# The opening of an attention + SwiGLU + max-out kernel: its stages in one written order

## The chip, the cores and the metric

One NeuronCore of a Trainium2 chip. The metric is the device time of the kernel on that core, in microseconds (us): the median over runs. Engines: PE (TensorE: matmuls, transposes), DVE (VectorE), ACT (ScalarE), POOL (GpSimd), SP (SyncE, which here only issues DMA transfers).

## The reference

```python
def _attn_ref(q, k, v):            # 4 batches, 8 heads, 576 positions, head size 64
    scores = (1 / sqrt(D)) * q @ k.T
    rel = pos[:, None] - pos[None, :]
    mask_local = (rel >= 0) & (rel < 32)                       # heads 0 to 3
    mask_strided = (rel >= 0) & (pos[None, :] % 32 == pos[:, None] % 32)   # heads 4 to 7
    attn = softmax(where(mask, scores, -1e9))
    return attn @ v
x = attn_out.transpose(0, 2, 1, 3).reshape(2304, 512)
x = (silu(x @ w_gate) * (x @ w_val)) @ w_out                   # 512 -> 1536 -> 512
return max(x @ w1, x @ w2, x @ w3) @ w_out2                    # 512 -> 768 -> 512
```

The inputs and weights are 32-bit floats; the weights arrive as 64-bit words, of which the kernel makes 32-bit floats itself.

## The kernel before, in words

**The whole.** The 2304 tokens are 72 rows of 32. A first stage works on five chunks of rows (`ROWS`: 16, 14, 14, 14, 14 rows, chunk c = 0 to 4): attention writes a chunk of x, then for each of `NF` = 12 slices f of the hidden width come a gate product (`emit_gate`), a value product (`emit_val`) and an output product (`emit_out`, one slice behind). A second stage does the max-out products from memory. To keep precision, PE works on pairs: a number is split into a high part (rounded, fp32r) and a low part (the rest), and `product` (lines 522 to 527) makes three matmuls of two pairs: high x high (line 525), high x low (526), low x high (527). A gate or value product of chunk 0 is 4 contraction slices (`k`; 0 and 1 hold the local heads, 2 and 3 the strided ones) x 3 = 12 matmuls of 128x512. For chunk 0 the gate uses tanh (line 548) and the output product plain fp32 (line 575); later chunks use Silu.

**Weights.** `order` lists 36 tiles g0, v0, g1, v1, o0, g2, v2, o1, ... (gate, value, output of slice f). A tile is loaded as raw 64-bit words (`load`, line 159, 512 KB, four buffers `raw_p`), converted (`convert`: two passes on ACT, lines 170 and 171; two on POOL, 172 and 173; two on DVE, 174 and 175) and split (`split_w`: high part on ACT, line 147, low part on DVE, line 150; v and o tiles are also written to memory for the later chunks). `weight_step` does one load, one conversion and one split; it is called `LEADW` times before chunk 0's products and three times in each of chunk 0's slices.

**The opening.** Chunk 0's attention is eight blocks (line 780 on): four of strided heads (blocks 0 to 3, 384 KB of loads each), four of local heads (blocks 4 to 7, 512 KB each). A block goes through `scores` (PE, line 311), `softmax` (on DVE masked reductions, line 323; on ACT four exponentials, line 327; on DVE the inverse of the sums, 330 and 331; on POOL the scaling, 332), `transpose` (PE, line 337; the eviction on ACT, 340, or DVE, 342) and `pv` (PE, line 351; then the high part of x on ACT, 357, and its low part on DVE, 359). A strided block has two units, and each is written into x by an operation of its own. After the eight blocks come the first weight steps, and already the first two blocks of chunk 1 (`loct` tiles, scores in line 315). Chunk 1's and 2's attention is spread over the slices of chunk 0 (`fill`); chunk 2's strided rows are done on DVE (`Unit.qk`, lines 437 and 440).

**What sets the order.** The kernel is written as a program, and a scheduler that models the engines' times chooses each engine's order from it when the kernel is built; `tc.issue_after` ties an instruction behind another. Before, one such tie keeps the reductions of the early blocks in the order of the blocks. The PSUM bank pool `gv` has two buffers for gate and value products: a gate product of f + 1 needs the bank that DVE's gate operation of f (line 549) has read last.

## Time and profile before

| | |
|---|---|
| median of 3 runs | 835.55 us (834.53 to 835.9) |
| the profiled execution | 833.92 us, of which its span is 832.1 |
| PE busy | 801.3 us, 96% of the span |
| DVE, ACT, POOL busy | 537.1, 368.0, 249.7 us |
| DMA moved | 202.84 MB, mean 244 GB/s |
| chain of work that ended last | PE 67%, DVE 10%, DMA 4%, ACT 4% |

The profile is one execution; its times are from the start of its span. "Busy" is time in which an engine had an instruction; instructions overlap a little, so the distance between two starts is often shorter than one duration. "Idle before <- X" says what ended the idle time in front of an instruction.

### The profile page before, as it was taken

What the parts mean: (1) busy time and instruction counts of PE and PEld (TensorE: products, weight loads), DVE (VectorE), ACT (ScalarE), POOL (GpSimd) and SP (SyncE); (2) the same over time, 40 slices, a digit from 0 to 9 for tenths busy, and PEclk for the clock granted to TensorE, in tenths of its full rate; (3) what the DMA queues carried; (4) which work ended last, traced back from release to release, by engine and by line L of the source; (5) the groups of instructions that cost most, each with busy time, mean ns of one, the idle gap of its engine ahead of it and who ended that gap; (6) DMA issues with size and microseconds to landing.
All of it is one profiled execution on the core that took longest, in us unless ns stands there. A gap on an engine that the chain in (4) does not pass through costs nothing.

```text
span 832.1 us, 12634 instructions
## 1 busy us (share of the span) xinstructions
PE 801.3 (96%) x4404; PEld 708.2 (85%) x4404; DVE 537.1 (65%) x1094; ACT 368.0 (44%) x834; POOL 249.7 (30%) x252
## 2 busy tenths in 40 slices
PE   4799999999999999899999999999999999999997
PEld 3666666688998889898899999999999989989986
DVE  2888889985956799979996573714644344614440
ACT  4967676334453744726542443523244122512321
POOL 1546655011231233412332465511222031402110
PEclk9999999999999999999999999999999999999999
DMA  8779989976574898577769899798666374744502
GB/s 224 230 229 337 308 270 322 386 235 205 174 239 169 248 297 298 175 262 237 260 217 353 270 374 365 230 386 339 229 246 220 137 242 177 263 155 173 194 0 76
DMA packets 73895, 202.84 MB, mean 244 GB/s; under 512 B 8584, under 2 KB 37896, under 8 KB 70248
## 3 DMA queue, kind: packets, MB, share of 16 engines
q1 hardware_dynamic: 73688, 201.91, 70.9%
q8 instruction: 35, 0.57, 0.3%
q14 instruction: 28, 0.23, 0.1%
q10 hardware_dynamic: 144, 0.13, 0.0%
HBM read 160.33 MB, written 41.68 MB: 243 GB/s over the span
## 4 chain that ended last, share of the span: by engine, by line
PE 67%; DVE 10%; DMA 4%; ACT 4%; issue 3%; SPq 1%; POOL 0%; DVEq 0%; ACTq 0%
PE ps_a L634 13%; PE ps_z L708 8%; PE ps_c L634 7%; PE ps_v L525 4%; PE ps_v L527 4%; PE ps_v L526 4%; PE ps_y L525 4%; PE ps_y L526 4%; PE ps_y L527 4%; PE ps_g L525 3%; PE ps_g L526 3%; PE ps_g L527 3%; PE ps_b L634 3%; DVE pr L437 1%; DVE pr L459 1%
## 5 line engine op out<-in xcount | busy, mean ns | idle before, releaser
L150 POOL TENSOR_TENSOR hl<-ht,hh 128x448 fp32r<-128x448 f32 x48 | 59.8, 1247 | 202.4 <-ACT hh L147 183.5
L150 POOL TENSOR_TENSOR hl<-t,hh 128x384 fp32r<-128x384 f32 x36 | 37.5, 1045 | 207.0 <-ACT hh L147 166.9
L634 PE MATMUL ps_a<-yhT,wr 128*128 128x384 f32 x324 | 94.5, 338 | 2.5 <-ACT s L648 2.5
L525 PE MATMUL ps_g<-xh,wh_g 128*128 128x448 f32 (+1 forms) x240 | 91.9, 383 | 4.0 <-DVE ht L549 2.7
L525 PE MATMUL ps_v<-xh,w_v 128*128 128x448 f32 (+1 forms) x240 | 90.9, 379 | 2.3 <-DVE ht L556 2.3
L526 PE MATMUL ps_g<-xl,wh_g 128*128 128x448 f32 (+1 forms) x240 | 89.5, 373 | 1.5 <-DVE xl L359 1.5
L527 PE MATMUL ps_v<-xh,w_v 128*128 128x448 f32 (+1 forms) x240 | 89.2, 372 | 0.0
L526 PE MATMUL ps_v<-xl,w_v 128*128 128x448 f32 (+1 forms) x240 | 89.1, 371 | 0.0
L527 PE MATMUL ps_g<-xh,wl_g 128*128 128x448 f32 (+1 forms) x240 | 89.0, 371 | 0.0
L648 ACT ACTIVATE s<-ps_a 128x384 f32<-128x384 f32 x81 | 39.3, 490 | 98.2 <-PE ps_a L634 98.0
L526 PE MATMUL ps_y<-hl,w_o 128*128 128x448 f32 x192 | 70.6, 368 | 0.0
L172 POOL TENSOR_SCALAR raw<-raw 128x512 f32<-128x512 f32 x60 | 55.7, 930 | 49.3 <-ACT w L170 26.6
L527 PE MATMUL ps_y<-hh,w_o 128*128 128x448 f32 x192 | 70.4, 366 | 0.0
L147 ACT ACTIVATE hh<-ht 128x448 fp32r<-128x448 f32 x48 | 27.7, 578 | 90.1 <-DVE ht L556 84.9
L708 PE MATMUL ps_z<-wo2t,hh 128*128 128x512 f32 x216 | 64.8, 392 | 0.9 <-ACT osb L726 0.7
L525 PE MATMUL ps_y<-hh,w_o 128*128 128x448 f32 x192 | 65.5, 370 | 0.1
L556 DVE SCALAR_TENSOR_TENSOR ht<-ht,ps_v 128x448 f32<-128x448 f32 (+1 forms) x60 | 37.6, 626 | 40.6 <-PE ps_v L527 25.4
L634 PEld LDWEIGHTS ps_a<-yhT,wr 128*128 128x128 f32 x324 | 59.7, 188 | 3.8 <-ACT s L648 3.2
L174 DVE SCALAR_TENSOR_TENSOR w<-w,raw 128x512 int32<-128x512 int32 x60 | 44.1, 738 | 17.1 <-POOL raw L172 9.2
L525 PEld LDWEIGHTS ps_g<-xh,wh_g 128*128 128x128 f32 x240 | 45.1, 188 | 11.5 <-DVE ht L549 4.4
L634 PE MATMUL ps_a<-ylT,wr 128*128 128x384 f32 x162 | 54.8, 338 | 0.0
L525 PEld LDWEIGHTS ps_v<-xh,w_v 128*128 128x128 f32 x240 | 45.1, 188 | 7.8 <-DVE ht L556 3.2
(134 smaller groups left out, 1880.6 us busy)
## 6 DMA issues: line engine op xcount, KB each, us to landing
wr<-wsdr SPq DMA_DIRECT2D x27, 1792.0 KB, 7.5
raw<-in_w_dram SPq DMA_DIRECT2D x60, 512.0 KB, 5.2
w_v<-wvdr SPq DMA_DIRECT2D x48, 512.0 KB, 4.5
w_o<-wodr SPq DMA_DIRECT2D x48, 512.0 KB, 4.7
wsdr<-whi SPq DMA_DIRECT2D x27, 256.0 KB, 3.6
wvdr<-w_v SPq DMA_DIRECT2D x12, 512.0 KB, 4.4
wodr<-w_o SPq DMA_DIRECT2D x12, 512.0 KB, 6.1
wsdr<-w SPq DMA_DIRECT2D x18, 256.0 KB, 3.5
```

The costliest lines, as they stand in the source:

```text
L147: a = nc.scalar.activation(hi, src, AF.Copy)
L150: return a.ins, lo_eng.tensor_tensor(lo, src, f32(hi), ALU.subtract).ins
L172: nc.gpsimd.tensor_scalar(f32(hi), f32(hi), -0.0, 1.0, ALU.mult, ALU.mult)
L174: nc.vector.scalar_tensor_tensor(w, w, 3, hi, ALU.logical_shift_left, ALU.bitwise_xor)
L437: eng.tensor_tensor(pv, self.k[:, 0:i + 1, :], self.q[:, r:r + 1, :].to_broadcast([128, i + 1, D]), ALU.mult)
L525: nc.tensor.matmul(ps, wh, xh, start=first, stop=False)
L526: nc.tensor.matmul(ps, wh, xl, start=False, stop=False)
L527: nc.tensor.matmul(ps, wl, xh, start=False, stop=last)
L556: m = nc.vector.scalar_tensor_tensor(t, t, 1.0 if c > 0 else 0.5, ps[:, :n], ALU.mult, ALU.mult).ins
L634: nc.tensor.matmul(ps, wts[:, c, a, ks], y[k][b], start=first and k == q == 0, stop=k == 1 and q == 2, skip_group_check=True,)
L648: nc.scalar.activation(s, self.a, AF.Copy)
L708: nc.tensor.matmul(z[j], a[:, ts], w[:, f, b], start=f == q == 0, stop=f == NF2 - 1 and q == 2)
```

## The change

The stages of a block and of a weight tile become steps of their own (`least`, `exps`, `inverse`, `normalise`, `turn`, `evict`, `outputs`, `high`, `low`; `size`, `rounding`, `sign`, `clamp`, `shift`, `rounded`, `high_w`, `low_w`). A string `OPENING` lists the steps of the eight blocks, of the loads, of the first five weight tiles (indices 0 to 4: g0, v0, g1, v1, o0) and of the first gate product, one letter a step, and within `tc.manual_schedule()` they are issued in that order. The first gate product is made in two halves: contraction slices 2 and 3 (`g0`), then 0 and 1 (`g1`). `LEADW` falls from 8 to 5: with the five tiles of the string, as many tiles are converted (11) and split (10) ahead of chunk 0's slices in the program as before. The two units of a strided block are written into x by one operation each for the high and the low part, in chunk 0 and chunk 1 (chunk 1's products are then 56 columns wide and not 64). The tie between the early reductions goes; a new one puts the first `qk` of chunk 2 behind the last low part issued before it.

```diff
-LEADW = 8
+LEADW = 5
...
+OPENING = """
+l0 k0 l1 l2 l3 l4 r0 l5 l6 l7 r1 r2 r3 S0 M0 E0 S1 R0 M1 N0 S2 E1 T0 M2 V0 R1 S3 E2 N1 P0 M3 T1 H0
+R2 E3 L0 S4 N2 T2 M4 V1 a0 R3 P1 V2 N3 E4 c0 T3 P2 s0 V3 R4 S5 H1 t0 r4 q0 P3 L1 N4 H2 M5 H3 T4 L2
+E5 S6 L3 d0 M6 h0 R5 V4 S7 o0 E6 P4 N5 M7 g0 E7 R6 N6 T5 q2 T6 R7 V5 a1 N7 H4 P5 s1 V6 L4 q1 T7 c1
+P6 H5 t1 V7 L5 a2 P7 d1 H6 c2 a3 L6 H7 s2 h1 L7 s3 q3 g1 t2 a4 o1 q4 d2 c3 h2 s4 t3 o2 d3 c4 h3 t4
+o3 d4 h4 o4
+"""
+FIRST = 5
...
-    def convert(key):
-
-        raw = raws.pop(key)
-        hi, lo = raw[:, :, 1], raw[:, :, 0]
+    def size(key):
+        nc.scalar.activation(f32(words(key)[1]), f32(raws[key][:, :, 1]), AF.Abs, scale=2.0 ** -80)
+
+    def rounding(key):
+        nc.scalar.activation(words(key)[0], raws[key][:, :, 0].bitcast(U32), AF.Copy, scale=2.0 ** -29)
+
+    def sign(key):
+        hi = f32(raws[key][:, :, 1])
+        nc.gpsimd.tensor_scalar(hi, hi, -0.0, 1.0, ALU.mult, ALU.mult)
+        eng.tensor_scalar(w, w, W_MAX, W_MIN, ALU.min, ALU.max)
+
+    def shift(key):
         nc.vector.scalar_tensor_tensor(w, w, 3, hi, ALU.logical_shift_left, ALU.bitwise_xor)
+
+    def rounded(key):
+        q, w = made.pop(key)
         nc.vector.tensor_tensor(w, w, q, ALU.add)
         cvt[key] = f32(w)
+    def convert(key):
+        for step in (size, rounding, sign, clamp, shift, rounded):
+            step(key)
+
+    def high_w(key):
...
+        nc.scalar.activation(wt[key][0], cvt[key], AF.Copy)
+
+    def low_w(key, lo_eng):
         w32 = cvt.pop(key)
-        split(*wt[key], w32, nc.scalar, lo_eng)
+        hi, lo = wt[key]
+        lo_eng.tensor_tensor(lo, w32, f32(hi), ALU.subtract)
...
         def softmax(self, norm_eng):
-            sm, mx, sums, ng = self.sm, self.mx, self.sums, 2 * self.nu
-            with ExitStack() as tied:
-                if early_order[0] is not None and self.early:
-                    tied.enter_context(tc.issue_after(early_order[0]))
-                for g in range(ng):
-                    early_order[0] = nc.vector.tensor_tensor_reduce(
-                        sm[:, g], self.s[:, g], self.masks[g // 2], -SCALE, 3.0e38, ALU.add, ALU.min, mx[:, g:g + 1]
-                    ).ins
-            for g in range(ng):
+            self.least()
+            self.exps()
+            self.inverse()
+            self.normalise(norm_eng)
+
...
-            parts = list(self.dst(ps[:, :2 * nu * QB].rearrange("p (a m) -> p a m", a=2)))
-            for hi, lo, src in parts:
+            self.parts = list(self.dst(ps[:, :2 * nu * nq].rearrange("p (a m) -> p a m", a=2)))
+
+        def high(self):
+            for hi, lo, src in self.parts:
                 nc.scalar.activation(hi, src, AF.Copy)
-            for hi, lo, src in parts:
-                nc.vector.tensor_tensor(lo, src, f32(hi), ALU.subtract)
+
+        def low(self):
+            for hi, lo, src in self.parts:
+                last_low[0] = nc.vector.tensor_tensor(lo, src, f32(hi), ALU.subtract).ins
...
-            for u, n in enumerate(g):
-                r0 = min(n * nr, STRIDE - nr)
-                su = src[:, :, u * QB:u * QB + nr * rows].rearrange("p a (r i) -> p a r i", i=rows)
-                for c, i0, i1, o in pieces(b * NI, b * NI + rows):
-                    def part(t):
-                        t = t[:, 2:4, :width(c)].rearrange("p a (i r) -> p a r i", r=STRIDE)
-                        return t[:, :, r0:r0 + nr, i0:i1]
-
-                    xh, xl = x_tile(c)
-                    yield part(xh), part(xl), su[:, :, :, o:o + i1 - i0]
-
-        return Block(srcs, (g[0], g[0]), rows * nr, [smask[b]] * len(g), dst, early)
+            su = src.rearrange("p a (r i) -> p a r i", i=rows)
+            for c, i0, i1, o in pieces(b * NI, b * NI + rows):
+                def part(t):
+                    t = t[:, 2:4, :width(c)].rearrange("p a (i r) -> p a r i", r=STRIDE)
+                    return t[:, :, g[0] * nr:(g[-1] + 1) * nr, i0:i1]
+
+                xh, xl = x_tile(c)
+                yield part(xh), part(xl), su[:, :, :, o:o + i1 - i0]
+
+        return Block(srcs, (g[0], g[0]), rows * nr, [smask[b]] * len(g), dst, early, rows * nr)
...
             steps[s0].append(lambda blk=blk: (blk.scores(), blk.softmax(eng)))
             steps[s0 + 1].append(lambda blk=blk: blk.transpose(nc.scalar))
             steps[s0 + 2].append(blk.pv)
+        def queued(step, n, r, eng):
+            if not (c == 2 and n == 0 and r == 0):
+                return step(r, eng)
+            with tc.issue_after(last_low[0]):
+                step(r, eng)
...
-                steps[s0 + (2 * r // u.n)].append(lambda u=u, r=r: u.qk(r, eng))
+                steps[s0 + (2 * r // u.n)].append(lambda n=n, u=u, r=r: queued(u.qk, n, r, eng))
...
+        return silu(c, f, ps)
+
+    def silu(c, f, ps):
+        n = width(c)
...
-        nc.sync.dma_start(cst, shape_consts)
-        for i, blk in enumerate(blocks):
-            blk.load()
-            if i in RAW_AT:
-                step_load(n_load[0] + 1)
-        lag = 4
-        for i in range(len(blocks) + lag):
-            if i < len(blocks):
-                blocks[i].scores()
-                blocks[i].softmax(nc.gpsimd)
-            if len(blocks) - 2 <= i < len(blocks):
-                step_cvt()
-            if i >= lag:
-                blocks[i - lag].transpose(nc.vector if i % 3 == 2 else nc.scalar)
-                blocks[i - lag].pv()
-        step_split(nc.gpsimd)
-        step_split(nc.gpsimd)
+        gate = []
+
+        def gate_part(ks):
+            if not gate:
+                gate.append(gv.tile([128, 512], F32, name="ps_g", tag="gv"))
+            (xh, xl), (wh, wl), ps = xt[0], wt["g", 0], gate[0][:, :width(0)]
+            for k in ks:
+                c = slice(k * 128, (k + 1) * 128)
+                product(ps, wh[:, c], wl[:, c], xh[:, k, :width(0)], xl[:, k, :width(0)], k == NK // 2, k == NK // 2 - 1)
+
+        def evictor(i):
+            return nc.vector if i % 3 == 2 else nc.scalar
+
...
+            "g": lambda i: gate_part(range(NK // 2, NK) if i == 0 else range(NK // 2)),
+        }
+        with tc.manual_schedule():
+            for step in OPENING.split():
+                steps[step[0]](int(step[1:]))
+        n_cvt[0] = n_split[0] = FIRST
...
-            t = emit_gate(c, f)
+            t = emit_gate(c, f) if s else silu(c, f, gate[0])
```

In the order that the scheduler makes of it, ACT has 36 loads of its function table where there were 30; the six more lie behind chunk 0. Three places of the opening, in the orders of the instructions before and now (line numbers are each kernel's own):

SP, the loads of blocks 2 to 4 (`qe`, `ke`, `ve`) and of the first raw weight tile (`raw`). Before:

```order
L299 DMA qe_162<-in_st0q_dram 128x256
L300 DMA ke_164<-in_st0k_dram 128x256
L301 DMA ve_163<-in_st0v_dram 64x512
L159 DMA raw_170<-in_w1_dram 128x1024
L299 DMA qe_172<-in_st0q_dram 128x256
L300 DMA ke_174<-in_st0k_dram 128x256
```

Now:

```order
L335 DMA ve_165<-in_st0v_dram 64x512
L333 DMA qe_172<-in_st0q_dram 128x256
L334 DMA ke_174<-in_st0k_dram 128x256
L335 DMA ve_173<-in_st0v_dram 64x512
L333 DMA qe_180<-in_earq_dram 128x256
L334 DMA ke_182<-in_lock_dram 128x384
L335 DMA ve_181<-in_locv_dram 96x512
L168 DMA raw_188<-in_w1_dram 128x1024
```

The raw tile has moved behind blocks 3 and 4.

PE, from the last blocks to the first value product (lines 345/311 scores, 388/337 transposes, 409/351 outputs, 349/315 scores of chunk 1, 592 to 594/525 to 527 products). Before:

```order
L351 MATMUL ps_a_491<-qe_188,ve_189 64x64 x8
L337 MATMUL ps_a_519<-cst_105,sme_208 96x128 x4
L315 MATMUL ps_a_820<-loct_814 128x96 x4
L351 MATMUL ps_a_508<-qe_196,ve_197 64x64 x8
L351 MATMUL ps_a_525<-qe_204,ve_205 64x64 x8
L315 MATMUL ps_a_842<-loct_836 128x96 x4
L525 MATMUL ps_g_684<-xh_329,wh_g0_536 128x512
L525 MATMUL ps_v_714<-xh_329,w_v0_540 128x512
L526 MATMUL ps_g_684<-xl_330,wh_g0_536 128x512
```

Now:

```order
L409 MATMUL ps_a_455<-qe_180,ve_181 64x64 x8
L592 MATMUL ps_g_469<-xh_301,wh_g0_435 128x512
...
L594 MATMUL ps_g_469<-xh_301,wl_g0_436 128x512
L388 MATMUL ps_a_483<-cst_105,sme_194 96x128 x4
...
L349 MATMUL ps_a_815<-loct_809 128x96 x4
L409 MATMUL ps_a_537<-qe_206,ve_207 64x64 x8
L349 MATMUL ps_a_837<-loct_831 128x96 x4
L592 MATMUL ps_g_469<-xh_301,wh_g0_435 128x512
```

Six matmuls of the first gate product now stand ahead of block 5's transposes, six behind chunk 1's scores.

ACT, from the last high part of x on (lines 417/357), with the passes over raw tiles (179 and 182/170 and 171), weight high parts (215/147), exponentials of chunk 1's blocks (367/327) and the tanh (619/548). Before:

```order
L357 ACTIVATE xh_329<-ps_a_525 128x2x128
L327 ACTIVATE sm_838,stat_837<-sm_838,stat_837 128x96 x4
L147 ACTIVATE wh_g1_568<-w32_549 128x512
L170 ACTIVATE w32_575<-raw_556 128x512
...
L171 ACTIVATE q_602<-raw_572 128x512
L147 ACTIVATE w_v1_582<-w32_561 128x512
L548 ACTIVATE ht_697<-ps_g_684 128x512
```

Now:

```order
L417 ACTIVATE xh_301<-ps_a_537 128x2x128
L215 ACTIVATE w_v0_555<-w32_500 128x512
L182 ACTIVATE q_549<-raw_218 128x512
L179 ACTIVATE w32_568<-raw_390 128x512
L182 ACTIVATE q_567<-raw_390 128x512
L367 ACTIVATE sm_811,stat_810<-sm_811,stat_810 128x96 x3
L367 ACTIVATE sm_833,stat_832<-sm_833,stat_832 128x96 x3
L619 ACTIVATE ht_692<-ps_g_469 128x512
```

The tanh had all of chunk 1's early exponentials and three raw tiles ahead of it; now the fifth raw tile (`raw_390`) and six exponentials stand ahead of it. On DVE, in the same stretch, chunk 0's last low part now stands ahead of the reductions of the second chunk-1 block, and the shift and the low half of w_v0 (`w_v0_555`) behind them.

## Rows read from the trace of the kernel before

**Rows 1.** Busy time by stage: length, then PE, PEld, DVE, ACT, POOL, clock, DMA.

```profile
0.00:37.45 37.45, 22.15 (x305) 18.59 (x305) 19.21 (x108) 25.55 (x100) 12.28 (x21) 0.95 0.81 224
37.45:47.59 10.14, 6.88 (x32) 5.25 (x32) 10.11 (x26) 7.06 (x19) 5.42 (x6) 1.00 0.64 194
47.59:160.00 112.41, 110.39 (x543) 76.44 (x544) 98.97 (x197) 70.87 (x165) 53.47 (x58) 1.00 0.91 312
160.00:460.00 300.00, 296.88 (x1630) 265.84 (x1629) 243.12 (x498) 143.44 (x308) 80.23 (x77) 1.00 0.74 244
```

**Rows 2.** Waits of PE up to 47.6 us: in total, times, longest.

```profile
PE ps_a L311 <- DMA ke<-in_st0k_dram: 10.5, 4, 6.0
```

**Rows 3.** PE in order of time: start, duration, line, [idle before <- releaser].

```profile
39.70 0.50 PE L526 MATMUL ps_g<-xl,wh_g 128*128 128x512 f32 x1 [1.52 <-DVE xl L359]
...
42.33 0.39 PE L526 MATMUL ps_v<-xl,w_v 128*128 128x512 f32 x1
...
44.59 0.39 PE L527 MATMUL ps_v<-xh,w_v 128*128 128x512 f32 x1
...
47.59 0.50 PE L525 MATMUL ps_g<-xh,wh_g 128*128 128x512 f32 x1 [1.74 <-DVE ht L549]
...
58.25 0.50 PE L525 MATMUL ps_g<-xh,wh_g 128*128 128x512 f32 x1
```

**Rows 4.** The same: the scores of blocks 2 and 3.

```profile
9.17 1.12 PE L311 MATMUL ps_a<-ke,qe 64*64 64x64 f32 x16 [0.55 <-DMA ke<-in_st0k_dram]
13.82 1.12 PE L311 MATMUL ps_a<-ke,qe 64*64 64x64 f32 x16 [3.53 <-DMA ke<-in_st0k_dram]
```

**Rows 5.** ACT in order of time, opening.

```profile
7.38 0.35 ACT L327 ACTIVATE sme<-sme,state 128x64 f32<-128x64 f32 x1 [5.37 <-DVE state L323]
...
23.28 0.61 ACT L357 ACTIVATE xh<-ps_a 128x128 fp32r<-128x128 f32 x2
23.69 0.66 ACT L170 ACTIVATE w<-raw 128x512 f32<-128x512 f32 x1
24.26 0.67 ACT L171 ACTIVATE q<-raw 128x512 int32<-128x512 uint32 x1
...
28.19 0.36 ACT L327 ACTIVATE sme<-sme,state 128x96 f32<-128x96 f32 x1
...
28.55 0.57 ACT L340 ACTIVATE qe<-ps_a 64x512 f32<-64x512 f32 x1
...
37.00 0.39 ACT L357 ACTIVATE xh<-ps_a 128x256 fp32r<-128x256 f32 x1
```

**Rows 6.** DVE in order of time: low parts, a reduction, the shift of a weight.

```profile
22.76 0.71 DVE L359 TENSOR_TENSOR xl<-ps_a,xh 128x128 fp32r<-128x128 f32 x2 [0.73 <-ACT xh L357]
...
36.31 0.68 DVE L174 SCALAR_TENSOR_TENSOR w<-w,raw 128x512 int32<-128x512 int32 x1
...
37.69 0.25 DVE L323 CUSTOM_DVE_ANT_0 sm<-ps_a,cst 128x96 f32<-128x96 f32 x1
...
39.23 0.42 DVE L359 TENSOR_TENSOR xl<-ps_a,xh 128x256 fp32r<-128x256 f32 x1
...
43.77 1.09 DVE L174 SCALAR_TENSOR_TENSOR w<-w,raw 128x512 int32<-128x512 int32 x1
```

**Rows 7.** The last load of chunk 1's two early blocks; landing times of their six loads.

```profile
23.45 0.49 SPq L301 DMA_DIRECT2D loct<-in_locv_dram  x1
...
DMA to landing us min/median/max: 8.4/9.0/9.1
```

**Rows 8.** Busy time and clock around 31 us, columns as in rows 1.

```profile
26.00:31.00 5.00, 2.03 (x33) 1.39 (x32) 4.40 (x18) 4.71 (x18) 2.44 (x3) 1.00 0.78 196
31.00:34.50 3.50, 3.50 (x43) 3.35 (x37) 3.50 (x6) 3.50 (x9) 2.80 (x3) 0.52 0.73 248
```

**Rows 9.** Table loads in front of Silu (busy, mean ns); longest PE wait in 160 to 400.

```profile
L546 ACT ACT_TABLE_LOAD x15 | 19.2, 1283 | 4.2 <-PE ps_g L527 4.0
...
PE ps_v L525 <- DVE ht L556: 2.1, 1, 2.1
```

More of the change, by code (lines that the diff above doesn't have):

```diff
@@ L254, in tile_attention_swiglu_maxout, with __init__ @@
     early_banks = [0]
-    early_order = [None]
+    last_low = [None]
     class Block:
-        def __init__(self, src, at, nk, masks, dst, early=False):
+        def __init__(self, src, at, nk, masks, dst, early=False, nq=QB):
             self.src, self.at, self.nk, self.masks, self.dst = src, at, nk, masks, dst
-            self.nu = len(masks)
+            self.nu, self.nq = len(masks), nq
             self.early = early
@@ L508, in attention_steps @@
         s0 = 0
-        for u in units:
+        for n, u in enumerate(units):
             steps[s0].append(u.load)
@@ L527, in product, with linear @@
         nc.tensor.matmul(ps, wl, xh, start=False, stop=last)
-    def linear(ps, w, x, n):
+    def linear(ps, w, x, n, ks=range(NK)):
         xh, xl = x
-        for k in range(NK):
-            ks = slice(k * 128, (k + 1) * 128)
-            product(ps, w[0][:, ks], w[1][:, ks], xh[:, k, :n], xl[:, k, :n], k == 0, k == NK - 1)
+        for k in ks:
+            c = slice(k * 128, (k + 1) * 128)
+            product(ps, w[0][:, c], w[1][:, c], xh[:, k, :n], xl[:, k, :n], k == ks[0], k == ks[-1])
     hs = {}
@@ new lines, in tile_attention_swiglu_maxout @@
+        steps = {
+            "l": lambda i: blocks[i].load(),
+            "S": lambda i: blocks[i].scores(),
+            "M": lambda i: blocks[i].least(),
+            "E": lambda i: blocks[i].exps(),
+            "R": lambda i: blocks[i].inverse(),
+            "N": lambda i: blocks[i].normalise(nc.gpsimd),
+            "T": lambda i: blocks[i].turn(),
+            "V": lambda i: blocks[i].evict(evictor(i)),
+            "P": lambda i: blocks[i].outputs(),
+            "H": lambda i: blocks[i].high(),
+            "L": lambda i: blocks[i].low(),
+            "r": lambda i: step_load(i + 1),
+            "a": lambda i: size(order[i]),
+            "q": lambda i: rounding(order[i]),
+            "s": lambda i: sign(order[i]),
+            "c": lambda i: clamp(order[i]),
+            "t": lambda i: shift(order[i]),
+            "d": lambda i: rounded(order[i]),
+            "h": lambda i: high_w(order[i]),
+            "o": lambda i: low_w(order[i], nc.vector),
+            "k": lambda i: nc.sync.dma_start(cst, shape_consts),
+            "g": lambda i: gate_part(range(NK // 2, NK) if i == 0 else range(NK // 2)),
+        }
```

65 lines of the change are left out of this document (48 added, 17 removed).

## Prediction

> **What bounds the kernel now.** I read the stages first [rows 1]: from 47.59 us on PE is busy 110.39 of 112.41 us, and then 296.88 of 300; in the 37.45 us before, it is busy 22.15, and between 37.45 and 47.59 it is busy 6.88 of 10.14. So time can be gained in the opening, where PE waits, and after it a microsecond comes only from doing less on PE. The waits of PE up to there [rows 2] name the loads of the strided blocks first, 10.5 us. The order of time on PE [rows 3] gives marks, and shows DVE as what ended the last two waits: the first gate product (f = 0, 12 matmuls) runs without a break from 39.70, the value product's last matmul starts at 44.59, the gate product of f = 1 starts at 47.59 and that of f = 2 at 58.25. From 42.33 to 44.59 there are ten spacings: 0.226 us a matmul. The sum is the shift of these marks.
>
> **The change, part by part.**
>
> *Loads.* The first raw weight tile (512 KB, 524 kB in bytes) moves from behind block 2 to behind block 4. Block 2's scores start at 9.17 and block 3's at 13.82 after a wait of 3.53 [rows 4]. At the opening's 224 GB/s [rows 1] the tile is 2.3 us, so blocks 3 and 4 come 2.3 earlier; everything behind block 4 has the same bytes ahead of it and lands when it did. The constants' 220 KB pass behind block 0's loads: DVE's masks need both, so the first reduction starts as before.
>
> *ACT up to the last early high part.* ACT carries most in the opening: 25.55 us busy in the first 37.45 [rows 1], 24.3 of them after its table load (1.28, as in [rows 9]), between the first exponential at 7.38 and the end of the last high part at 37.39 [rows 5]; it idled 5.7. In the written order it has, before the last high part (H7): 3 exponentials less (0.36 each), one conversion pass less (0.57, from 23.69 to 24.26), one weight high part less (the same size, 0.57), one eviction more (0.57, some 0.5 from start to start), and four strided pairs of high parts as single operations (0.61 becomes the 0.39 of a 128x256 one, 0.22 less each) [rows 5]. That is 2.6 less: 21.7 us. Never idle, ACT would end H7 at 7.4 + 21.7 = 29.1; with the old idle time of 5.7, at 34.8. I take 2.5 of idle time, nearer the lower end, because 2.3 of the old idle is the load that moves and, as I judge, about 0.9 lay where a conversion stood ahead of an exponential: H7 ends at 31.6. DVE's low part follows with 0.42 [rows 6], ahead of the next chunk's reductions and no longer behind them: 32.0.
>
> *The gate product in halves.* Six of its twelve matmuls (the strided heads) run before block 5's transposes, in PE's idle time, if the first weight is split by then; its conversion goes first among weights on ACT and DVE. Six are left at 32.0: 6 x 0.226 = 1.4, end 33.4. Before, 39.70 + 12 x 0.226 = 42.4. Lead 9.0.
>
> *The value product.* Its third matmul needs the low half of w_v0, which on DVE stands behind the four reductions of the second next-chunk block (0.25 each, overlapped: 0.7) and one shift (0.68) and takes 0.68 itself [rows 6]: 32.0 + 2.1 = 34.1, then ten matmuls: 36.4. Before: 44.59 + 0.23 = 44.8. Lead 8.4.
>
> *The gate product of f = 1.* It needs its bank back, so DVE's gate operation of f = 0, behind ACT's tanh. The tanh now stands in ACT's queue behind both passes over the fifth raw tile and six exponentials. This tile is loaded behind the next chunk's two blocks, whose last piece is issued at 23.45 and lands 8.4 to 9.1 later [rows 7], 31.9 to 32.6; one tile more at 224 GB/s gives 34.2 to 34.9, and I take 34.4. Then 2 x 0.57 + 6 x 0.36 = 3.3 and the tanh 0.5: 38.2. DVE: gate operation, value operation of f = 0 and the low half of w_g1, three of about 0.65: 40.2. The third matmul of f = 1 waits for the last, ten follow: end 42.5. Before: 47.59 + 12 x 0.226 = 50.3. Lead 7.8.
>
> *To f = 2.* Between these marks PE runs nearly the same in both, four transposes more and a few small products less; the lead stays. From it I take 0.8 for DVE operations that run beside POOL: the same shift takes 0.68 in one place and 1.09 in another [rows 6], and two or three of those on this path will. **Sum: 7.0 us.**
>
> *What costs nothing.* The four merged pairs of the next chunk, and DVE's 8 x (0.71 - 0.42) = 2.3 us [rows 6] over all eight, lie in stretches in which DVE idles: 112.41 - 98.97 = 13.4 us between 47.59 and 160 [rows 1]. That idle time must also carry what is converted later: at the start of f = 2 DVE has done some two weight operations less than before, 1.3 us. The tie that holds chunk 2's first products behind chunk 1's low parts moves DVE work by a few us there, inside the same cover; if that cover were gone, each DVE operation would cost PE its 0.68. The transposes' evictions change engine once; they are in the ACT sum.
>
> Profiled execution: 833.92 - 7.0 = 826.9. The median of the runs is 1.6 above it, so I forecast **828.5 us** against 835.55. What can be told from no change is 0.2%, 1.7 us.
>
> **The clock.** The granted clock was at its lower level, 1.2 GHz, for nearly all of 31.0 to 34.5 (0.52 on average), after five microseconds in which PE was busy 2.03 [rows 8]; this stretch alone makes the 0.95 of the first 37.45 us [rows 1]. It fell on transposes and small products. Were the same stretch to fall on the second half-product and the value product, 3.4 us at half speed would lose 1.7 us. The Trainium skill, "TensorE: Matmul & The Clock Gate", section "Part 1: The HAM clock gate", calls the slow clock the default that activity releases; by that, products that come out of a sparse opening start slow. The trace agrees for 31 to 34.5; it does not agree at the start, where the clock reads full. In the written order PE has six large matmuls and nearly all of the small ones from 23 to 31, more than it had, so I count it as a rival and not in the sum.
>
> **The rivals.**
> 1. *The fifth raw tile lands in time.* Where DMA moves at the 312 GB/s of the later stage [rows 1], it lands before ACT asks (about 33), the tanh comes 1.4 earlier, and the lead at f = 2 is some 8.4 to 9.2: 826.7. For: the later stage's rate; against: 224 in the opening. 20%.
> 2. *The clock falls on the first large products:* 828.5 + 1.7 = 830.2. For it the rows above; against it the fuller PE. 15%.
> 3. *The chunk-0 stage becomes short of weights.* DMA is busy 0.91 of it at 312 GB/s [rows 1]. With PE 7 us earlier, one or two raw tiles more, up to 1.05 MB, must be moved within the stage; at 312 GB/s that is 3.4 us if DMA has no slack at all: 831.9. 15%. If DMA or the ring of four raw tiles paces the whole stage, the end of it does not move and the whole lead goes: about 835. Against: PE idles 2.0 us in that stage in all. 6%.
> 4. *Slower: the exponential/silu switches of the later stages.* In the new order ACT loads its table 36 times and not 30. Each load is 1.28 us in front of a silu or an exponential [rows 9]. Where a value product is over before ACT and DVE have freed its bank, PE waits; the longest such wait is 2.1 us [rows 9]. Six waits of 2.1 are 12.6: 835.55 - 7.0 + 12.6 = 841.2. It decides the sign from 8.7 us of new waits on, more than four of the six. Against: the 30 loads there now go with 3.1 us of PE idle time in 300 [rows 1]. 4%.
>
> **How the numbers follow.** The forecast itself (a gain of 5 to 9 us) has 40%, rival 1 20%, rival 2 15%, rival 3's first part 15%: these are faster, 90%. The lead given back is 6%: 4 of them within 0.2% and 2 still faster or slower by a little, which I leave in the same. Rival 4 has 4%. The range: the ACT bound of 29.1 would give 2.5 us more, 826.0, with a raw tile in time some 825.2; the upper end takes in rival 3's 831.9. The ACT bound of 34.8 (3.2 later) gives 831.7, inside it. Outside stay the lead given back, the slower case and combinations, under 20%. Range 825.2 to 831.9.
>
> **What would show each step.** In the profile after: block 3's scores near 11.5; six gate matmuls between 23 and 27 and the other six at about 32; the end of the value product near 36.4; ACT waiting for a raw tile near 33 to 34.4, ahead of six exponentials and the tanh; the gate product of f = 1 with a wait for DVE near 40; the gate product of f = 2 at 50 to 51.5 and not 58.25; after it the same PE work with 2 to 4 us of idle time between there and 460. The prediction is wrong if the mark of f = 2 moves by 7 and the time does not (rivals 3 or 4: the waits of PE after 60 us tell which), or if H7 is not over by 35 us: then the written order has a wait that my sum of ACT's durations does not hold.

## The result, and the profile after

| | before | after |
|---|---|---|
| median | 835.84 us (834.53 to 837.86, 5 runs) | 829.11 us (826.47 to 830.75, 5 runs) |
| ratio to before, 95% interval | | 0.9914 (0.9889 to 0.9940) |
| the profiled execution, its span | 833.92, 832.1 | 827.85, 826.0 |

The change makes the kernel 6.7 us faster; the forecast was 828.5. The profiled executions differ by 6.07 us. The same stages as in [rows 1], of the changed kernel:

```profile
0.00:37.45 37.45, 27.07 (x334) 21.04 (x334) 22.74 (x121) 29.49 (x111) 14.30 (x23) 1.00 0.89 253
37.45:47.59 10.14, 9.48 (x49) 6.23 (x49) 10.14 (x16) 7.82 (x15) 5.45 (x6) 1.00 0.74 241
47.59:160.00 112.41, 110.34 (x517) 74.64 (x516) 101.52 (x203) 68.74 (x162) 49.99 (x57) 0.98 0.92 319
160.00:460.00 300.00, 297.10 (x1643) 267.99 (x1642) 239.27 (x482) 151.54 (x310) 80.66 (x78) 1.00 0.73 240
```

PE has 4.9 us more work in the first stage and 2.6 more in the second, ACT 3.9 more in the first. The clock column reads 1.00 in the first stage (0.95 before) and 0.98 in the third (1.00 before); at the start of the span it cannot be taken at its word (see below, after_again). The marks of [rows 3], PE in order of time:

```profile
31.04 0.50 PE L592 MATMUL ps_g<-xh,wh_g 128*128 128x512 f32 x1
...
32.53 0.40 PE L594 MATMUL ps_g<-xh,wl_g 128*128 128x512 f32 x1
...
35.61 0.39 PE L594 MATMUL ps_v<-xh,w_v 128*128 128x512 f32 x1
...
36.95 0.47 PE L592 MATMUL ps_g<-xh,wh_g 128*128 128x512 f32 x1
...
38.32 0.50 PE L594 MATMUL ps_g<-xh,wl_g 128*128 128x512 f32 x1 [0.66 <-DVE wl_g L220]
...
40.49 0.39 PE L594 MATMUL ps_g<-xh,wl_g 128*128 128x512 f32 x1
...
49.27 0.50 PE L592 MATMUL ps_g<-xh,wh_g 128*128 128x512 f32 x1
...
157.59 0.45 PE L592 MATMUL ps_g<-xh,wh_g 128*128 128x448 f32 x1
```

The second half product is issued from 31.04 to 32.53, the value product ends with the matmul of 35.61, f = 1 runs from 36.95, with a wait in front of its third matmul, to 40.49, f = 2 starts at 49.27. The last row is chunk 1's first gate product. The same product in the kernel before:

```profile
163.87 0.77 PE L525 MATMUL ps_g<-xh,wh_g 128*128 128x448 f32 x1
```

Against the kernel before, the lead is 58.25 - 49.27 = 9.0 us at f = 2 and 163.87 - 157.59 = 6.3 at chunk 1. The span keeps 6.1 of it. So 2.7 us are given back inside the chunk-0 stage, and next to nothing behind it.

ACT in the opening, in order of time (the rows with idle time in front from the first exponential on, and the fifth raw tile's two passes):

```profile
6.27 0.35 ACT L367 ACTIVATE sme<-sme,state 128x64 f32<-128x64 f32 x1 [4.25 <-DVE state L359]
...
8.27 0.35 ACT L367 ACTIVATE sme<-sme,state 128x64 f32<-128x64 f32 x1 [0.57 <-DVE state L359]
...
11.10 0.59 ACT L393 ACTIVATE qe<-ps_a 64x512 f32<-64x512 f32 x1 [1.40 <-PE ps_a L388]
...
21.27 0.63 ACT L215 ACTIVATE wh_g<-w 128x512 fp32r<-128x512 f32 x1 [0.36 <-DVE w L200]
...
30.25 0.38 ACT L367 ACTIVATE sm<-sm,stat 128x96 f32<-128x96 f32 x1 [0.42 <-DVE stat L359]
...
30.63 0.36 ACT L417 ACTIVATE xh<-ps_a 128x256 fp32r<-128x256 f32 x1
...
31.98 0.67 ACT L179 ACTIVATE w<-raw 128x512 f32<-128x512 f32 x1
...
35.25 0.59 ACT L619 ACTIVATE ht<-ps_g 128x512 f32<-128x512 f32 x1
```

From 11.10 to the last high part at 30.63 ACT is idle twice, 0.36 and 0.42 us: in this execution it is the engine that sets the opening's length. The pass of 31.98 has no wait in front: the fifth raw tile is in time.

Where the 2.7 us went, by windows (columns as above):

```profile
140.10:141.20 1.10, 0.05 (x2) 0.05 (x2) 1.00 (x2) 1.10 (x3) 0.00 (x0) 1.00 1.04 425
141.20:142.30 1.10, 1.10 (x18) 0.99 (x19) 1.10 (x3) 0.84 (x2) 0.00 (x0) 0.92 1.04 425
142.30:145.60 3.30, 3.30 (x6) 1.76 (x6) 3.08 (x6) 1.09 (x2) 0.00 (x0) 0.51 1.04 421
145.60:147.50 1.90, 1.90 (x7) 0.82 (x5) 1.90 (x3) 0.00 (x0) 0.00 (x0) 1.00 1.01 409
```

PE stands still for 1.1 us (an eviction of a chunk-1 block waits on ACT behind a weight's high part, and that for DVE), does a string of products of 56 columns, and then runs 3.3 us at the lower level, 1.2 GHz, on large matmuls: at half speed some 1.6 us lost.

### The profile page after: what moved, and what is told of

Its sections match the earlier page's. It is cut to its first block, busy times and chain, and to the rows that moved or that the text cites. A ratio compares the mean times of both kernels' runs of the same rounds, so it can differ in the third digit from the quotient of the medians.

```text
span 826.0 us, 12610 instructions
## 1 busy us (share of the span) xinstructions
PE 802.5 (97%) x4404; PEld 706.1 (85%) x4404; DVE 538.4 (65%) x1085; ACT 376.6 (46%) x833; POOL 248.2 (30%) x252
## 4 chain that ended last, share of the span: by engine, by line
PE 67%; DVE 11%; DMA 5%; ACT 3%; issue 3%; SPq 1%; DVEq 0%; ACTq 0%
PE ps_a L705 13%; PE ps_z L779 9%; PE ps_c L705 6%; PE ps_v L592 4%; PE ps_v L594 4%; PE ps_v L593 4%; PE ps_y L592 4%; PE ps_g L592 4%; PE ps_y L594 4%; PE ps_y L593 4%; PE ps_g L593 4%; PE ps_g L594 4%; PE ps_b L705 3%; DVE pr L520 2%; DVE pr L498 1%
## 5 line engine op out<-in xcount | busy, mean ns | idle before, releaser
L156 ACT ACTIVATE hh<-ht 128x448 fp32r<-128x448 f32 x48 | 27.7, 578 | 83.2 <-DVE ht L627 81.8
L186 POOL TENSOR_SCALAR raw<-raw 128x512 f32<-128x512 f32 x60 | 50.9, 851 | 46.9 <-ACT w L179 41.6
L627 DVE SCALAR_TENSOR_TENSOR ht<-ht,ps_v 128x448 f32<-128x448 f32 (+1 forms) x60 | 37.6, 626 | 33.4 <-PE ps_v L594 24.4
L196 DVE SCALAR_TENSOR_TENSOR w<-w,raw 128x512 int32<-128x512 int32 x60 | 46.1, 772 | 11.4 <-POOL raw L186 8.6
```

The lines of the kernel that those rows point to most:

```text
L156: a = nc.scalar.activation(hi, src, AF.Copy)
L186: nc.gpsimd.tensor_scalar(hi, hi, -0.0, 1.0, ALU.mult, ALU.mult)
L196: nc.vector.scalar_tensor_tensor(w, w, 3, hi, ALU.logical_shift_left, ALU.bitwise_xor)
L627: m = nc.vector.scalar_tensor_tensor(t, t, 1.0 if c > 0 else 0.5, ps[:, :n], ALU.mult, ALU.mult).ins
```

## The experiments

Each group of runs was timed beside the kernel before on its own chip, so ratios are compared and not times. "Marks" are places of the profiled execution.

| kernel | median us (runs) | before beside it | ratio (95%) | f = 2 starts |
|---|---|---|---|---|
| whole_product | 834.84 (12) | 835.21 | 0.9993 (0.9973 to 1.0013) | 56.27 |
| parts_apart | 831.96 (12) | 835.21 | 0.9966 (0.9945 to 0.9986) | 50.18 |
| tile_early | 834.15 (12) | 835.21 | 0.9983 (0.9969 to 0.9997) | 53.80 |
| no_tie | 830.49 (6) | 835.21 | 0.9942 (0.9920 to 0.9965) | 51.16 |
| after_again | 828.40 (9) | 834.97 | 0.9927 (0.9903 to 0.9951) | 50.49 |
| whole_filler | 828.89 (6) | 834.97 | 0.9923 (0.9895 to 0.9952) | 50.77 |
| evict_dve | 826.26 (6) | 834.97 | 0.9909 (0.9881 to 0.9938) | 50.97 |
| qk_pool | 831.34 (12) | 834.97 | 0.9961 (0.9942 to 0.9980) | 49.90 |
| pace_c2 | 830.69 (6) | 834.59 | 0.9946 (0.9925 to 0.9967) | 51.03 |
| evict_pace | 828.49 (6) | 834.59 | 0.9910 (0.9889 to 0.9931) | 51.2 |
| before_merged | 838.66 (12) | 834.59 | 1.0043 (1.0022 to 1.0065) | 56.95 |

**The first gate product whole.**

```diff
-... P4 N5 M7 g0 E7 R6 ... s3 q3 g1 t2 ...
+... P4 N5 M7 E7 R6 ... s3 q3 g0 g1 t2 ...
```

> The change with its first gate product in one piece: the six matmuls of the strided heads stand directly ahead of the other six, nothing else moves. Theory (the product is on the path from 31 us on, six matmuls of 0.226 more stand there): the value product of f = 0 ends 1.0 to 1.4 us later than in the changed kernel, the gate product of f = 2 starts 1.0 us later (50.3 for 49.3), and the time is 0.7 to 1.4 above 829.1, about 830.1. Rival A (the later part of the chunk-0 stage gives leads back whatever they are): the mark of f = 2 moves by 1.0 and the time by less than 0.4. Rival B (with the six matmuls gone from 23 to 25 PE is too sparse and the clock falls on the products at 31, as it did in the kernel before): a further 1.7, about 831.8, and a granted clock near 0.5 in the three microseconds from 31 on.

The whole gain is gone, and f = 2 starts 7.0 us later than in the first execution of the changed kernel, 5.1 to 7.0 later than in the five executions of its opening that are listed below. Rival B shows, far bigger than priced. Windows of this kernel:

```profile
20.00:26.00 6.00, 4.49 (x80) 3.92 (x77) 5.41 (x33) 5.02 (x21) 1.12 (x1) 1.00 1.04 342
26.00:28.40 2.40, 0.94 (x7) 0.43 (x5) 1.23 (x5) 2.40 (x11) 1.24 (x2) 0.90 1.07 258
28.40:38.30 9.90, 9.89 (x72) 8.42 (x73) 6.07 (x20) 7.68 (x22) 4.92 (x8) 0.51 0.53 140
38.30:40.00 1.70, 1.70 (x11) 1.45 (x11) 1.70 (x5) 1.09 (x2) 0.97 (x2) 1.00 0.86 333
```

After 2.4 us in which PE is busy 0.94, everything up to 38.3 runs at 1.2 GHz: the last transposes and small products first, then half of the gate product. At half speed 9.9 us lose 4.9. The mean granted clock of its twelve runs is 0.985 to 0.992; of the three other variants of that group it is 0.994 to 1.000 (of the kernel before beside them 0.987 to 0.999). So low clock is common to all twelve, but where it lies is seen in this one profile only, and there three more stretches of 3.4 us follow, at 127, 345 and 680 us: half of its low time is behind the opening.

The clock is not all of it, and "nothing else moves" does not hold behind the written string: the scheduler chose another order there. ACT and PE of this kernel, then the tanh of the filler kernel that follows:

```profile
42.97 0.57 ACT L619 ACTIVATE ht<-ps_g 128x512 f32<-128x512 f32 x1
```

```profile
46.20 0.50 PE L592 MATMUL ps_g<-xh,wh_g 128*128 128x512 f32 x1 [2.88 <-DVE ht L620]
```

```profile
37.74 0.60 ACT L619 ACTIVATE ht<-ps_g 128x512 f32<-128x512 f32 x1
```

The gate product's last matmul starts at 39.74, but the tanh stands behind the passes over two more raw tiles and comes at 42.97, DVE's gate operation at 45.47, and the gate product of f = 1 waits 2.9 us for it. In the filler kernel, as in the changed kernel, one raw tile's passes and six exponentials stand ahead of the tanh.

**The same, with six products that compute nothing in the first half's place.**

```diff
-... P4 N5 M7 E7 R6 ...
+... P4 N5 M7 f0 E7 R6 ...
+            ps = gv.tile([128, 512], F32, name="ps_f", tag="gv")[:, :width(0)]
+            for k in range(NK // 2, NK):
+                product(ps, wh[:, c], wl[:, c], xh[:, k, :width(0)], xl[:, k, :width(0)], k == NK // 2, k == NK - 1)
```

> The gate product whole at the end, and at the place of its first half six products of the same size into a bank that nothing reads (they compute nothing of the output). Theory (what the early half is worth is that PE is kept busy and the clock stays at its upper level): no stretch below 0.9 between 26 and 40 us; the value product ends 1.4 us later than in the changed kernel and not 7, the time is 1.0 to 1.5 above the changed kernel's, about 830. Rival (the six matmuls at the end, the waits behind them and the different order of later work cost all of it, not the clock): the time is that of the whole product without these, within 1.0 of 834.8.

```profile
20.00:24.30 4.30, 2.19 (x36) 1.66 (x35) 4.27 (x24) 3.42 (x13) 0.00 (x0) 1.00 1.02 362
24.30:27.70 3.40, 3.33 (x21) 2.76 (x22) 1.86 (x13) 3.40 (x19) 1.95 (x2) 0.50 1.08 303
27.70:40.00 12.30, 11.96 (x108) 9.98 (x107) 10.24 (x33) 11.60 (x35) 6.94 (x10) 1.00 0.64 205
```

The time is the changed kernel's, 828.89 beside 828.40. Here too the clock falls, at 24.3, but on one block's products and the filler, and it is back at 27.7, 3.4 us later. The expectation of no stretch below 0.9 "between 26 and 40" is missed by this, and its 1.0 to 1.5 us too: the value product ends later, but f = 2 starts at 50.77 beside 50.49, because the gaps in front of f = 1 and of its third matmul (0.66 above; gone here) take up what the longer product costs. The forecast priced the early half as six matmuls fewer at the end, 1.4 us. In these two executions that is 0.3 us at f = 2, less than the mark moves from execution to execution (below). Work of this size in this place is worth 0.9993 - 0.9923 = 0.0070 +- 0.0035 of 835, 5.8 us +- 2.9, also where it computes nothing. Two things make that up. The clock: in the two profiles the opening loses 4.9 and 1.7 us to it, and over all runs the mean granted clock is 0.9892 and 0.9975, which over some 830 us is 6.9 us of clock lost more. And the scheduler's order: f = 1 waits 2.9 us in the whole product, as shown above, and not at all here. The run changes both at once, so the share of each is not shown. Nor does the early half rule out a low stretch: of the nine profiles that have it, two (pace_c2, 0.75 from 26 to 31 us, and evict_pace, 0.71) show one in the opening, of 3.4 us and over before 29; in all nine the products from 30 us on run at 2.4 GHz up to f = 2.

**The first raw tile back behind block 2.**

```diff
-l0 k0 l1 l2 l3 l4 r0 l5 ...
+l0 k0 l1 l2 r0 l3 l4 l5 ...
```

> The change with one DMA moved: the first raw weight tile is loaded behind block 2 again and not behind block 4; the order on PE, ACT, DVE and POOL is the same. Theory (its 2.3 us of transfer delays blocks 3 and 4, and ACT, in a fixed order, waits for their exponentials): block 3's scores start near 13.3 and not 10.99, ACT idles 1.0 to 1.7 us more, and the last high part, the mark of f = 2 and the time move by that: about 830.5. Rival (ACT's other work of that time is enough to cover it; the same bytes are ahead of all later loads): the last high part stays within 0.3 of 30.6 and the time within 0.4 of 829.1.

PE, ACT, DVE and POOL have the same orders; one DMA moves. PE's scores of block 3, then ACT's idle rows:

```profile
13.36 0.97 PE L345 MATMUL ps_a<-ke,qe 64*64 64x64 f32 x13 [2.50 <-DMA ke<-in_st0k_dram]
```

```profile
15.35 0.61 ACT L417 ACTIVATE xh<-ps_a 128x256 fp32r<-128x256 f32 x1 [2.54 <-PE ps_a L409]
...
20.92 0.59 ACT L393 ACTIVATE qe<-ps_a 64x512 f32<-64x512 f32 x1 [1.16 <-PE ps_a L388]
...
23.91 0.61 ACT L417 ACTIVATE xh<-ps_a 128x256 fp32r<-128x256 f32 x1 [0.96 <-PE ps_a L409]
```

The theory's place and time are right (13.36), its price is not: in a fixed order ACT waits three times, 4.7 us in all, the last high part starts at 35.14 (30.63 to 32.50 in the changed kernel), and nearly all of the gain goes: f = 2 comes 2.6 to 4.5 later for 2.3 us of transfer. The ratio is larger than after_again's by 0.0056 +- 0.0028, 4.7 us +- 2.3. The price is not the load's alone: all three waits are for PE, and in this execution PE's small products are slow for longer than in the changed kernel (16 matmuls of 64x64 take 1.12 us at 18.68, 0.68 at 15.80 in after_again). Whether the later load brings that about, no run separates.

**The changed kernel again.**

> The changed kernel itself, once more, beside the three that follow. If the opening's fixed order leaves ACT no slack, its marks shift with the landing of the first loads from execution to execution: the first half product starts between 23 and 25 us, and the times spread over some 4 us as in the first five (826.5 to 830.8), about a median of 0.991 of the kernel before. If the spread is from the later clock stretches alone, the marks in the opening repeat within 0.3 us.

The spread is that of the first case, its cause only in part. Besides this one, three kernels have the changed kernel's opening unaltered, so that it is seen five times (block 4's scores are 16 matmuls of 64x96):

| execution | block 3's scores start | block 4's scores take | first half product | last high part | f = 2 | lead at f = 2 |
|---|---|---|---|---|---|---|
| after | 10.99 | 0.88 | 23.05 | 30.63 | 49.27 | 9.0 |
| qk_pool | 10.24 | 1.21 | 23.6 | 31.22 | 49.90 | 8.4 |
| after_again | 10.98 | 1.45 | 24.3 | 31.83 | 50.49 | 7.8 |
| pace_c2 | 10.61 | 1.53 | 24.4 | 32.36 | 51.03 | 7.2 |
| no_tie | 11.05 | 1.54 | 24.9 | 32.50 | 51.16 | 7.1 |

The same instructions in the same order move by 1.9 us. The start of block 3's scores, which wait for their load, does not sort the executions; the time that PE takes for block 4's scores does. The fastest and the slowest:

```profile
13.26 0.88 PE L345 MATMUL ps_a<-ke,qe 64*64 64x96 f32 x16
```

```profile
13.93 1.54 PE L345 MATMUL ps_a<-ke,qe 64*64 64x96 f32 x16
```

PE thus works slowly from the start until a moment that differs: the traces' first entry of the granted clock, at its full level, stands at 12.4, 13.8, 15.1, 14.9 and 16.8 us, in the order of the table. The clock column counts the time before it as 1.00, so a 1.00 at the start of a span is no measurement. The loads add to it: in after_again ACT waits 0.79 us for the first raw tile, for which it did not wait in the first execution:

```profile
16.07 0.67 ACT L179 ACTIVATE w<-raw 128x512 f32<-128x512 f32 x1 [0.79 <-DMA raw<-in_w_dram]
```

It also tells what the 2.7 us were. Its stage at 140 us has the same gap (PE waits 1.1 for the eviction on ACT), but no low clock behind it:

```profile
142.20:145.60 3.40, 3.40 (x11) 1.93 (x11) 3.18 (x7) 1.30 (x3) 0.00 (x0) 1.00 1.04 420
```

From f = 2 to chunk 1 it takes 156.29 - 50.49 = 105.8 us, as the kernel before does (105.6); the first execution took 108.3. So 1.6 of those 2.5 us are the clock's; 0.4 is a wait of PE for a load that after_again does not have, the rest I have not found. The lead of 7.8 is kept: the span is 824.9, 7.2 under that of before.

**The strided parts in two operations again.**

```diff
-            su = src.rearrange("p a (r i) -> p a r i", i=rows)
-            for c, i0, i1, o in pieces(b * NI, b * NI + rows):
+            for u, n in enumerate(g):
+                m = nr * rows
+                su = src[:, :, u * m:(u + 1) * m].rearrange("p a (r i) -> p a r i", i=rows)
+                for c, i0, i1, o in pieces(b * NI, b * NI + rows):
```

> The change with each strided block's high and low part in two operations again (128x128 each), in the same written order. Theory (ACT works without a break from 11.1 us to the last high part, so what is added there is added to the path): four blocks with 0.22 more on ACT: the last early high part starts 0.9 us later (31.5 for 30.6), the gate product of f = 2 0.5 to 0.9 later, the time 0.5 to 0.9 above 829.1. Rival (ACT has room, its order only looks unbroken): the marks stay within 0.2 and the time within 0.4. Rival on the later stage: the four strided blocks of chunk 1 also cost PE something, then the time rises by more than the mark of f = 2 does.

The marks cannot settle it: 31.51 and 50.18 lie inside the five executions above. The time says that the merge is worth something: against after_again the ratio is larger by 0.0039 +- 0.0032, 0.6 to 5.9 us, so that it is worth more than its 0.9 is likely but not shown. Its profile has both late stretches of low clock (143 and 338 us). Whether the merge makes these likelier stays open.

**The merge alone, in the kernel before.**

```diff
-            for u, n in enumerate(g):
-                r0 = min(n * nr, STRIDE - nr)
...
+            su = src.rearrange("p a (r i) -> p a r i", i=rows)
+            for c, i0, i1, o in pieces(b * NI, b * NI + rows):
```

> The kernel before with the merged strided parts alone (one high and one low part a block, in the old, scheduled order). Theory (ACT bounds the opening, four pairs at 0.22 each): the first gate product starts 0.5 to 0.9 us earlier than 39.7, the time falls by 0.5 to 0.9, a ratio of 0.999. Rival A (in the old order ACT has 5.7 us of idle time, waiting for loads and for DVE, which take the gain): no change. Rival B (DVE gains too, 2.3 us over eight blocks, and the last low part is what the first product waited for): up to 2 us, 0.9975.

None of the three: it is slower, by 0.0043, 3.6 us. The opening does what the theory said, and more: the first product goes on from 38.64 (39.70 before), f = 1 starts at 45.83 and f = 2 at 56.95, 1.3 earlier. But chunk 1 starts at 165.63, 1.8 later. DVE in order of time, then the only wait of PE from 138 to 170 us, and two windows:

```profile
146.52 2.29 DVE L436 TENSOR_TENSOR pr<-stk,stq 128x960 f32<-128x960 f32 x2 [3.05 <-DMA stq<-in_strd_dram]
...
152.56 0.67 DVE L548 SCALAR_TENSOR_TENSOR ht<-ht,ps_g 128x512 f32<-128x512 f32 x1
```

```profile
PE ps_g L524 <- DVE ht L548: 3.1, 1, 3.1
```

```profile
150.00:155.00 5.00, 1.88 (x7) 1.44 (x7) 5.00 (x8) 0.00 (x0) 0.00 (x0) 0.93 1.01 332
155.00:160.00 5.00, 5.00 (x21) 4.09 (x21) 5.00 (x8) 1.41 (x3) 0.00 (x0) 0.73 1.05 334
```

The scheduler, given shorter operations, orders chunk 1's and 2's attention otherwise in chunk 0's slices. Chunk 2's first product now stands on DVE before its load has landed: DVE idles 3.05 us (a wait that the kernel before does not have), the gate operation behind it comes at 152.56, PE waits 3.1 us, and the clock falls. The opening, too, has more low clock than before (0.70 from 26 to 37.45, against 31 to 34.5 in [rows 8]). A part that shortens ACT's and DVE's work made the kernel slower, and what the profile shows of it (1.7 us of span, of the 3.6 between the medians) comes from the order that was chosen with it.

**Without the tie of chunk 2's first products.**

```diff
-            if not (c == 2 and n == 0 and r == 0):
+            if True:
```

> The change without the tie that holds chunk 2's first products on DVE behind chunk 1's last low part. The opening is the same, so the mark of f = 2 stays at 49.3. Theory (DVE's idle time in the chunk-0 stage covers the order of that work): the time stays within 0.4 of 829.1. Rival (the products of 1.2 us and their reductions come ahead of chunk 1's low parts, and the first gate product of chunk 1 waits for these): 1 to 3 us more, about 831, with a wait of PE for DVE near 158 to 166 us. Second rival: the tie itself costs, and without it the kernel is 0.5 to 1.5 faster.

0.9942, beside 0.9914 and 0.9927 with the tie: the intervals overlap, and neither a cost of 1 to 3 us nor a gain shows. From f = 2 to chunk 1 it takes 107.4 us at full clock, 1.6 more than after_again; PE waits 1.3 us there for a load of a later block. Inconclusive; the products do not wait for their load here, so the tie had nothing to hold back. Its profile shows the other place where the clock falls, at the end of chunk 2. First this kernel, then after_again:

```profile
336.00:338.00 2.00, 0.30 (x1) 0.31 (x2) 2.00 (x4) 0.33 (x1) 0.00 (x0) 0.92 0.90 354
338.00:341.30 3.30, 3.30 (x10) 2.94 (x10) 3.30 (x16) 3.25 (x5) 1.87 (x2) 0.53 0.75 285
```

```profile
336.00:338.00 2.00, 1.79 (x9) 1.65 (x10) 2.00 (x5) 1.79 (x2) 1.09 (x1) 1.00 0.80 287
338.00:341.30 3.30, 3.30 (x18) 3.00 (x17) 3.30 (x17) 3.26 (x11) 0.81 (x2) 1.00 0.79 284
```

In all 13 profiles PE waits there for a value operation on DVE, 1.1 to 2.1 us. Where the wait is 1.8 or more (eight profiles), the clock falls behind it in five, for some 3.3 us; where it is 1.2 or less (five), in none.

**Two attempts on the late stages.** `qk_pool` gives chunk 2's first multiplications to POOL:

```diff
+        def early_eng(n):
+            return nc.gpsimd if c == 2 and n == 0 else eng
```

> The change with the multiplications of chunk 2's first unit (four of about 1.2 us, on DVE in the last 20 us of the chunk-0 stage) moved to POOL, which is idle there. Theory (the lead is given back where DVE is full, between 130 and 160 us): the stage from the gate product of f = 2 to chunk 1's first gate product shortens from 108.3 to 106 or less, and the time falls by 1 to 2.5. Rival A (DVE operations beside POOL are slower, 1.09 for 0.68, and the reductions wait for POOL): no gain, within 0.5. Rival B (what gives the lead back is the low clock after PE's gap at 140 us, and the gap is ACT's order): the gap and the loss stay.

Slower than the changed kernel, 0.9961. PE's wait for the eviction on ACT grows from 1.1 to 2.8 us, the clock falls behind it (0.83 from 140 to 150), and the stage takes 158.3 - 49.9 = 108.4. The theory that fewer DVE products there return the lead falls; rival B's gap and loss stay, and grow. Of rival A, DVE's reductions wait 0.9 and 1.3 us for POOL's products. `pace_c2` spreads chunk 2's weight steps otherwise:

```diff
-PACE = [0, 0.7, 1.4, 1.4, 3.1]
+PACE = [0, 0.7, 1.75, 1.4, 3.1]
-            if c > 0 and f < PACED:
+            if c > 0 and f < (8 if c == 2 else PACED):
```

> The change with one number and one bound of the pacing altered: chunk 2's 14 steps of second-stage weights are spread over its first eight gates and not over ten, so DVE has fewer of them in chunk 2's last gates, near 330 us, where it is full (19.9 of 20 us) and PE waits 1.2 to 2.1 us for a value operation behind its queue. Theory (that wait, and the low clock that followed it in five of the eight executions of the new order profiled so far, are what spreads the times): the wait falls below 1 us, no stretch below 0.9 follows it, the time is 0.5 to 2 us under the changed kernel's, a ratio of about 0.991 to the kernel before, with fewer times above 830. Rival (DVE is full in the earlier gates as well, 18 of 20 us, and the wait moves there): no change, ratio 0.992 to 0.994.

(The profiles up to then were nine, not eight.) The wait is 1.2, no better than in after_again, and the ratio 0.9946: the rival.

**Two early evictions on DVE, alone and with that pacing.**

```diff
-            return nc.vector if i % 3 == 2 else nc.scalar
+            return nc.vector if i in (2, 4, 5, 7) else nc.scalar
```

> The change with the transposes of early blocks 4 and 7 evicted by DVE and not by ACT (blocks 2 and 5 already are), in the same places of the order. Theory (ACT alone sets the opening's length, DVE has some 1.4 us idle in each five): ACT has two operations of 0.5 less before the last high part, which starts 0.7 to 1.0 earlier, and the time falls by 0.5 to 1.0. Rival (DVE in a fixed order waits for PE's transposes at these places and holds up the reductions and low parts behind them): the last high part comes no earlier, the time is the same or up to 1 us longer.

The last high part starts at 32.00, behind 0.77 us of waiting for PE, a wait of the rival's kind. But 32.00 lies inside the 30.63 to 32.50 of the changed kernel's executions, so one profile cannot tell a shift of 0.7 to 1.0. The median is the best of all, 826.26, and its profile (822.4) has no low stretch in the clock column; the scheduler's order behind the opening differs too. The interval holds the changed kernel's ratio.

> The two edits together: early blocks 4 and 7 evicted by DVE, and chunk 2's paced steps over eight gates. If both are worth what their profiles suggest, 2 to 3 us under the changed kernel: ratio 0.988 to 0.990. If the first one's better median was chance, the ratio is that of the pacing alone, 0.991 to 0.993.

0.9910 (0.9889 to 0.9931): between the two cases, so no version here is shown to beat the change.

## Why the prediction was right, and where it was not

*Loads.* Block 3's scores: forecast near 11.5, measured 10.99. tile_early shows that with this one DMA 2.6 to 4.5 us of the lead come or go, perhaps in part through PE's slow start. The first reduction, and with it the first exponential, started 1.1 earlier than before (6.27, not 7.38), which "starts as before" missed.

*ACT up to the last high part.* Forecast to end at 31.6, with 2.5 us of idle time; measured 30.63 + 0.36 = 31.0, with 0.57 + 1.40 + 0.36 + 0.42 = 2.75 idle. Over five executions the end is 31.0 to 32.9, with 2.75 to 4.2 of idle time. So the path is right, and the mark in part by luck: the start that came 1.1 earlier paid for idle time that was taken too small.

*The gate product in halves.* The marks are right (forecast from 32.0 to 33.4; measured from 31.0 to 32.8), **the reason is not**. The step counted six matmuls, 1.4 us; beside the filler, with the later large products at full clock, they gain nothing that can be told (0.3 at f = 2). What counts is that PE has work there: without any, 5.8 us +- 2.9 go, through the clock and through the scheduler's order. The forecast had the clock as a rival that costs 1.7 and counted the fuller PE against it; it did not see that without that fuller PE nearly the whole gain falls. (It also read the row at 39.70 as the product's first matmul; that had run at 37.45, which moves its 42.4 by less than 0.1.) The Trainium skill, "TensorE: Matmul & The Clock Gate", section "Part 1: The HAM clock gate", calls the slow clock the default that activity releases. whole_product agrees in that its large products find the lower level behind a sparse stretch. The start of the span agrees too, which the forecast denied: its clock column reads 1.00 in the kernel before, but the 16 matmuls of 64x64 at 9.17 and 13.82 take 1.12 us each time [rows 4], and 16 others of that size later 0.68:

```profile
21.39 0.68 PE L351 MATMUL ps_a<-qe,ve 64*64 64x64 f32 x16 [0.78 <-DVE qe L342]
```

*The value product.* Forecast end 36.4, measured 35.61 + 0.23 = 35.8, with w_v0's low part on DVE from 32.71 as named.

*The gate product of f = 1.* This term was wrong in size. The fifth raw tile was to land at 34.4; ACT took it at 31.98 without a wait, so the tanh started at 35.25 and not 37.7, and f = 1 ended at 40.7 and not 42.5: lead 9.6, not 7.8. Rival 1's condition, given 20%, came true, in all five executions; its time, 826.7, did not. In the opening DMA moved 253 GB/s and not 224.

*To f = 2.* 49.27, lead 9.0, not 7.0; over five executions 7.1 to 9.0. The 0.8 for DVE beside POOL was about right in size (9.6 to 9.0), and by luck. From the end of f = 1 to f = 2, in this kernel and in the kernel before (columns as in [rows 1]):

```profile
40.72:49.27 8.55, 8.55 (x52) 5.05 (x51) 8.55 (x13) 6.66 (x12) 4.59 (x6) 1.00 0.91 297
```

```profile
50.45:58.25 7.80, 7.80 (x53) 4.89 (x53) 4.90 (x9) 5.64 (x11) 4.81 (x6) 1.00 0.69 256
```

PE is busy without a break in both, so no wait for DVE took it. What is more on PE is the four transposes, 0.57 us from start to start, which the forecast named and priced at nothing.

*What costs nothing.* Wrong for the chunk-0 stage. The lead does not simply stay: in the profiled execution 2.7 us were given back there, 1.6 by a stretch of low clock behind a 1.1 us gap. The forecast looked for the clock only in the opening. That 828.5 came out so near is luck: a lead at f = 2 that was 2.0 too small was not charged with the 2.9 us that were lost from there to the end. In after_again both are nearer to the forecast: lead 7.8, span 7.2 shorter.

*Rivals 3 and 4.* Neither shows: from f = 2 to chunk 1 after_again needs what the kernel before needs, and ACT's 36 table loads go with 2.9 us of PE idle time from 160 to 460 (3.1 before).

## What to carry to other kernels

Where one engine works without a break through a hand-written order, a transfer that comes late in front of it can cost more than its own length; look for the idle rows of that engine, not of PE. Price an early piece of PE work by the clock that the next large products will find, test it with products that compute nothing in the same place, and compare the order behind it too. At the start of a span read PE's speed from how long equal matmuls take, not from the clock column. A scheduler that orders later work from its model of the times can turn a shorter operation into a longer kernel: judge each piece in the order in which it will run.

## What the runs showed that I had not expected

- How long the clock stayed low differed: 9.9 us in whole_product and 6.8 in before_merged, in their openings, but 3.3 to 3.5 us everywhere else. What PE did meanwhile does not explain it: transposes and small products came first in whole_product, and also in the stretch of 3.5 us in the kernel before [rows 8]; large products followed at once in others of 3.3 to 3.4 (changed kernel at 142, no_tie at 338). The cause stays open.
- After the same gap, in the same order, the clock falls in one execution and not in the next (142 us: after and after_again).
- PE's slow start ends at another time in each execution of the same order, 12.4 to 16.8 us. The Trainium skill, "TensorE: Matmul & The Clock Gate", section "Part 1: The HAM clock gate", says that the slow start varies between runs of one kernel; the five executions agree. With the low stretches later on this is the likely source of the spread of 5 us in the changed kernel's times (826.5 to 831.5 in 14 runs): their mean granted clock, which does not count the start, goes with the times at a correlation of -0.7, so it accounts for about half of their variance.
